# Two attention layers and two gated MLPs on one core: queries written over their normalised tile, a P ring of 48 places, other ranks for norms and spatial sums

## The chip, the core and the metric

The kernel runs on one core of a Trainium2 chip. The metric is the device time of one execution in microseconds. The core has five instruction streams: TensorE (PE, with its weight loads shown as PEld), VectorE (DVE), ScalarE (ACT), GpSimd (POOL) and SyncE (SP), which starts the DMAs. They meet only at semaphores.

## The reference

Two layers, each an attention with 32 query heads of 16 that share one key and one value head, and a gated MLP whose gate mixes the 2048 tokens. `x` is 2048 x 512, bf16.

```python
def _A_ref(x, wq, wk, wv, wo):
    q = (x @ wq).reshape(B, S, H, Dh).transpose(0, 2, 1, 3)
    k = x @ wk
    v = x @ wv
    scores = jnp.einsum('bhqd,bkd->bhqk', q, k) * Dh ** (-0.5)
    p = _softmax(scores, axis=-1)
    o = jnp.einsum('bhqk,bkd->bhqd', p, v)
    return o.transpose(0, 2, 1, 3).reshape(B, S, H * Dh) @ wo

def _B_ref(x, w_in, w_sp, b_sp, w_out):
    z = _gelu(jnp.einsum('bsd,df->bsf', x, w_in))
    z1 = z[..., :Fh].copy()
    z2 = _layernorm(z[..., Fh:], axis=-1)
    g = jnp.einsum('ts,bsf->btf', w_sp, z2) + b_sp[None, :, None]
    return jnp.einsum('bsf,fd->bsd', z1 * g, w_out)

x = x + _A_ref(_layernorm(x), wq, wk, wv, wo)
x = x + _B_ref(_layernorm(x), w_in, w_sp, b_sp, w_out)
# the same two lines once more
```

## The kernel before

The program is written by a planner that runs on the host when the kernel is built. Work is cut into tasks, each with an engine, a modelled duration, dependencies and a priority (a smaller number goes first). `Sched` and `Kernel.run` walk through modelled time: whenever an engine is free, its `step_` function picks a ready task by priority, and that fixes the engine's instruction order and its semaphore waits. The chip then runs the five fixed streams. So a constant of the planner doesn't cost anything by itself; it changes the order of instructions.

**Attention.** The tokens are 16 tiles of 128 (t). `attn_inputs` makes, for each tile, a layer norm, its transpose, keys and values (`keys`, L766 on) and queries (`queries`, L795). The transposed norm `xnT(t)` lies in z1, in rows that the MLP fills only later: `z1[:, t // 4, 0:4, o:o + 128]`. The query matmuls (L800) read it, and an eviction (L810 on VectorE, L811 on ScalarE) writes the scaled queries to a ring Q of 8 tiles. A query job for t of 2 and more may start only when the layer's ramp is over (`full`), and for t of 8 and more only when all score blocks of tile t - 8 have been issued (`later`).

Queries are worked off in eight chunks (`CHUNKS`, 128 to 512 tokens), in 32 units of 512 columns for a layer. A unit meets 16 key tiles with 4 row groups each, so a layer has 2048 score blocks of 128 x 512. `issue_pack` (L1244) sends up to four blocks as one pack of score matmuls (L1286), each to a PSUM bank of its own; there are eight banks. A block then goes one of two ways. On ScalarE, `pick_exp` joins one or two blocks whose banks and whose places in the P ring are neighbours into one exponential (L1494): a single is 128x512, a pair 128x1024. Or on VectorE (task "A", priority 1.0): L1408 reads the bank and writes a first integer tile, and GpSimd or VectorE make two more from it (L1413), so that such a block takes three places of P. `issue_pack` gives VectorE a share of 0.32 or 0.34 of the blocks. All these tiles live in the ring `Pb` of `NPS` = 40 places, until the matmuls of P and V (L1549) have read them; `do_pv` sends those in rounds of four column groups, and `pv_hurry` sends them with fewer once under 8 places are free.

`pack_ready` (L1206) decides whether a pack may go: with fewer than four blocks only if ScalarE's modelled backlog is no more than `ACT_LOW`, and with no fewer than `FILL_MIN` (in layer 1's ramp `FILL_R`, with a backlog of 0). Score packs come first on TensorE, then P·V rounds, then everything else by priority.

**What lies between the score packs.** When a chunk is through, `attn_out` (L844) normalises, multiplies with wo, adds to X and makes the second layer norm (`ln`, statistics L638 and L639 on VectorE, then GpSimd), with priority 0.8. `mlp_in` forms a batch for each group of chunks: gelu on ScalarE (L1022, L1077) between two table loads, from matmuls L1017 and L1063. `spatial` (L1102) runs the token mix in five passes; passes 0 to 3 add up in `gp` with matmuls L1124 and an addition on VectorE (L1132, priority 1.05), 28 jobs a pass. The last pass and the output matmuls (L1162, L1170, L1191, L1195) come after all score blocks of the layer.

So the run has five stages: a start, the attention of layer 0 with the passes between its score packs, the change of layers, the attention of layer 1, and a tail.

Of the kernel before, what the change touches and what calls it, by code (L numbers as in the profile page):

```python
# [292 lines left out]
class Attn:  # L293

    def __init__(self, K, layer):
        self.K = K
        self.layer = layer
        self.kdep, self.vdep, self.qdep = {}, {}, {}
        self.nxt = 0
        self.started = False  # L300
        self.full = False
        self.ugs = []
        for ci, (q0, nq) in enumerate(CHUNKS):
            ng = 512 // nq
            for g0 in range(0, 4, ng):
                for half in range(2):
                    self.ugs.append(UG(ci, q0, nq, g0, ng, half))
        self.blocks = []
        nrot = K.NROT[layer]
        for kt in range(NT):  # L310
            for u in self.ugs[:nrot]:
                self.blocks += [(u, kt, j) for j in range(4)]
        for u in self.ugs[nrot:]:
            self.blocks += [(u, kt, j) for kt in range(NT) for j in range(4)]
        self.nrot = nrot
        self.end = None
        self.last_block = {}
        for i, (u, kt, j) in enumerate(self.blocks):
            for t in range(u.q0 // P, (u.q0 + u.nq) // P):
                self.last_block[t] = i + 1  # L320
        self.chunk_ugs = {}
        for u in self.ugs:
            self.chunk_ugs.setdefault(u.ci, []).append(u)
# [69 lines left out]
class Kernel:  # L393
# [1 line left out]
    SCORE_CAP = 6  # L395
    WSP_FROM = 25000
    W_FROM = 45000
    NPS = 40
    QT = 8
    PV_FREE = 6  # L400
    KT_ACT = 16
    CREDIT = 2
# [22 lines left out]
    PE_LINE = 5000  # L425
    WARM = 0.6
    FILL_MIN = 2
    FILL_R = 4
    NOID = (False, True)
    PTT = 1.8  # L430
    ACT_LOW_R = 0
    PV_R = 0
    RAMP_SHARE1 = 0.0
    ACT_LOW = 1300
    POOL_MAX = 1400
    DVE_MAX = 1500
    DVE_HIGH = 1800
# [41 lines left out]
    def alloc(self):  # L479
        nc = self.nc  # L480
        ps = self.es.enter_context(nc.psum_tensor("ps_all", [P, 4096], FP32))
        self.ps32 = ps[:].rearrange("p (b c) -> p b c", c=512)
        self.ps16 = ps[:].bitcast(BF16).rearrange("p (b c) -> p b c", c=1024)
        self.ident = self.sb([P, P], BF16, "ident")
        self.zero = self.sb([P, 32], BF16, "zero")
        self.ident16 = self.sb([P, P], FP16, "ident16")
        self.X = self.sb([P, NT, D], BF16, "X")
        self.kT = self.sb([P, 2, S], BF16, "kT")
        self.NV = 1 + len(TERMS)
        self.V = self.sb([P, self.NV, NT, 32], BF16, "V")  # L490
        self.wq = self.sb([P, KD, D], BF16, "wq")
        self.wk0 = self.sb([P, KD, DH], BF16, "wk0")
        self.wk = self.sb([P, KD, 8, DH], BF16, "wk")
        self.wv = self.sb([P, KD, DH], BF16, "wv")
        self.wo = self.sb([P, 4, D], BF16, "wo")
        self.w_in = self.sb([P, KD, FF], BF16, "w_in")
        self.w_out = self.sb([P, NF, D], BF16, "w_out")
        self.Q = self.sb([P, 4, self.QT * P], BF16, "Q")
        self.xnT2 = self.sb([P, 1, KD, 512], BF16, "xnT2")
        self.z2 = self.sb([P, 8, FH], BF16, "z2")  # L500
        self.z1 = self.sb([P, 4, NF, 512], BF16, "z1")
        self.gp = self.sb([P, 4, NF, 512], FP16, "gp")
        self.wstr = self.sb([P, self.NWS, 512], BF16, "wstr")
        self.bspc = self.sb([P, 512], BF16, "bspc")
        self.oT = self.sb([P, 3, 512], BF16, "oT")
        self.o_norm = self.sb([P, 4, 512], BF16, "o_norm")
        self.onT = self.sb([P, 4, 4, P], BF16, "onT")
        self.rden = self.sb([P, 2, 32], FP32, "rden")
        self.NXN = 4
        self.xn = self.sb([P, self.NXN, D], BF16, "xn")  # L510
        self.ln_st = self.sb([P, NT, 6], FP32, "ln_st")
        self.ln_mv = self.sb([P, NT, 2], FP32, "ln_mv")
        self.ln_rs = self.sb([P, NT, 1], FP32, "ln_rs")
        self.ln_nm = self.sb([P, NT, 1], FP32, "ln_nm")
        self.nm2 = self.sb([P, NT, 1], FP32, "nm2")
        self.st2 = self.sb([P, NT, 2, 6], FP32, "st2")
        self.mv2 = self.sb([P, NT, 2], FP32, "mv2")
        self.rs2 = self.sb([P, NT, 1], FP32, "rs2")
        self.masks = self.sb([P, 2], FP32, "masks")
        self.dummy = self.sb([P, 4], FP32, "dummy")  # L520
        self.vw = self.sb([P, self.NV], FP32, "vw")
        self.mhalf = self.sb([P, 1], FP32, "mhalf")
        self.Pb = self.sb([P, self.NPS, 512], BF16, "Pb")
        self.Pi = self.Pb[:].bitcast(I16)
# [33 lines left out]
    def misc_cap(self):  # L558
        if self.batch is not None:
            return 2  # L560
        if not self.attn_on():
            return 7
        return 1 if self.attns[self.ai].full and self.pe_line() < self.CAP_LINE else 2

    def score_cap(self):
        return self.SCORE_CAP if self.attns[self.ai].full else 4

    def job(self, prio, pieces, consumers, tag, kind="misc", batch=None, spare=0, only=None):

# [222 lines left out]
        made, outs = self.job(prio, [(kf, c_mm(8, 96), [dep, self.t_wk, self.ldv])], [mk, mkv], "KV")  # L792
        return made, outs[0], outs[1]

    def queries(self, A, t, dep, war, prio):  # L795
        def qf(e, b, lo, hi):
            ins = None
            for g in range(lo, hi):
                for kd in range(KD):
                    ins = e.matmul(self.ps32[:, b, g * P:(g + 1) * P], self.wq[:, kd, g * P:(g + 1) * P], self.xnT(t, kd),  # L800
                                   start=(kd == 0), stop=(kd == KD - 1))
            return ins

        def mk(last, bank):
            o = self.Q[:, :, t % self.QT * P:(t % self.QT + 1) * P]

            def src():
                return self.ps32[:, bank(), :].rearrange("p (g c) -> p g c", g=4)
            return Task(None, None, None, [last] + list(war), prio - 0.5, tag="qev",
                        alts={"dve": (c_ps(512), lambda e: e.tensor_scalar(o, src(), QSCALE, None, op0=ALU.mult)),  # L810
                              "act": (c_act(512), lambda e: e.activation(o, src(), ACTF.Copy, scale=QSCALE))})  # L811
        def later():

            if self.ai >= len(self.attns) or not self.attns[self.ai].full:
                return False
            return t < self.QT or A.nxt >= A.last_block[t - self.QT]
        made, outs = self.job(prio, [(lambda e, b: qf(e, b, 0, 2), c_mm(8, 128), [dep, self.ldq]),
                                     (lambda e, b: qf(e, b, 2, 4), c_mm(8, 128), [])], [mk], "Q", only=later if t >= self.Q_LATE else None)
        return made, outs[0]

    def attn_inputs(self, layer, xdeps):
# [5 lines left out]
        for t in range(NT):  # L827
# [6 lines left out]
            made, kout, vout = self.keys(t, ev, war, pr)  # L834
            A.kdep[t] = [kout]
            A.vdep[t] = [vout]
            m, q = self.queries(A, t, ev, war, pr + 0.01 if t < 2 else 4 + 0.05 * t if t < self.QT else 3 + 0.02 * t)
            A.qdep[t] = q
            self.xnT_use[t] = made + m
        self.attns.append(A)  # L840
# [3 lines left out]
    def attn_out(self, A, ci):  # L844
# [127 lines left out]
        buf = 0  # L972
        base = next(CHUNKS[g[0]][0] for g in GROUPS if ci in g)
        evs = []
        allx = self.ln(tl, [xnew[t] for t in tl], 0.8, pool=not last)
        for a in range(0, ntl, 2):
            pair = tl[a:a + 2]
            xs = allx[a:a + 2]
# [123 lines left out]
    def spatial(self, B, pi, final):  # L1102
# [5 lines left out]
        for tc in range(4):  # L1108
# [6 lines left out]
            else:  # L1115
# [4 lines left out]
                for f in range(NF):  # L1120
# [8 lines left out]
                    def mk(lp, bank, f=f, tc=tc):  # L1129
                        src = self.bspc[:] if pi == 0 else self.gp[:, tc, f, :]  # L1130
                        dps = [lp, lb] + self.gp_free if pi == 0 else [lp, B.gpw[(tc, f)]]
                        return Task("dve", c_ps(512), lambda e: e.tensor_tensor(  # L1132
                            self.gp[:, tc, f, :], self.ps32[:, bank(), :], src, ALU.add), dps, 1.05, tag="gp")
                    made, outs = self.job(self.SP_PRIO + 0.1 * pi, pcs, [mk], "SP%d" % pi)
                    B.gpw[(tc, f)] = outs[0]
                    if pi == 0:
# [69 lines left out]
    def pack_ready(self):  # L1206
# [2 lines left out]
        A = self.attns[self.ai]  # L1209
        av = self.banks.avail()  # L1210
        room = min(4, len(av), self.score_cap() - self.score_held)
        low = self.ACT_LOW if A.full or A.layer == 0 else self.ACT_LOW_R
        if room < (self.FILL_MIN if A.full or A.layer == 0 else self.FILL_R) or room < 4 and self.act_backlog() > low:
            return None
        blks = []
        deps = []
# [6 lines left out]
        if not blks or len(blks) < room and len(blks) < 4 and A.nxt + len(blks) < len(A.blocks) and self.act_backlog() > low:  # L1223
            return None
        return A, blks, deps, av

    def act_backlog(self):
        return max(0.0, self.s.free["act"] - self.s.t) + 450.0 * len(self.act_q)
# [15 lines left out]
    def issue_pack(self, A, blks, deps, bs):  # L1244
# [36 lines left out]
        def fn(e):  # L1281
            ins = None
            for i, (u, kt, j) in enumerate(blks):
                o = u.q0 % (self.QT * P)
                q = self.Q[32 * j:32 * j + 32, u.g0:u.g0 + u.ng, o:o + u.nq]
                ins = e.matmul(self.ps32[:, jb[i].i, :], self.kT[32 * j:32 * j + 32, u.half, kt * P:(kt + 1) * P], q,  # L1286
                               tile_position=(32 * j, 0), start=True, stop=True)
            return ins
# [338 lines left out]
    def pack_due(self):  # L1627
# [15 lines left out]
        d = max(t, s.free["dve"]) + 130  # L1643
        known += [d + 603 * (i + 1) for i in range(sum(1 for _, _, k in s.arm["dve"] if k.start is None and k.tag == "A"))]
        known.sort()
        e2 = known[self.FILL_MIN - 1] if len(known) >= self.FILL_MIN else t + 600
        e4 = known[3] if len(known) > 3 else t + 1e5
        dry = max(t, s.free["act"]) + 450.0 * len(self.act_q) - self.ACT_LOW
        w = min(e4, max(e2, dry))
        if w > t:  # L1650
            s.event(w)
# [274 lines left out]
```

## Time and profile before

| | us |
|---|---|
| median of five runs | 1583.33 |
| lowest and highest | 1580.65, 1587.83 |
| the profiled execution | 1583.63 |
| its span, first to last instruction | 1581.5 |
| TensorE busy | 1490.6 (94%) |
| ScalarE busy | 1431.3 (90%) |
| VectorE busy | 1385.9 (88%) |
| GpSimd busy | 1043.6 (66%) |
| score matmuls L1286, 4096 | 591.9 |
| P·V matmuls L1549, 6668 | 520.9 |
| spatial matmuls L1124, 840 | 214.1 |
| query matmuls L800, 512 | 41.2 |
| VectorE score blocks L1408, 1286 | 840.1 |
| spatial sums L1132, 224 | 151.5 |

Busy time is the union of an engine's instructions, so overlapping ones are counted once. A group's line gives busy time and mean duration of one, then the idle time of the engine just before its instructions and whom it waited for. The granted TensorE clock was 0.986 in the mean, lower only in the first 75 us. ScalarE's instructions overlap when they follow each other directly, so the mean duration of an exponential is more than the time that one more of them takes.

### The profile page before, as it was taken

The page shows a single profiled execution, that of the slowest core. Times are in us where ns is not written, and L with a number is a line of the kernel's source. Part 1 is how long each engine was busy: PE and PEld are TensorE (multiplying, and loading weights), DVE is VectorE, ACT ScalarE, POOL GpSimd, SP SyncE. Part 2 cuts the span into 40 slices and gives each one's busy share as a digit, 9 for nine tenths or more (in the row PEclk, how much of TensorE's full clock was granted, in tenths as well). Part 3 has the DMA queues.
Part 4 walks back from the last instruction along what each step waited for, and adds up shares of the span by engine and source line. Part 5 has one row for each costly group of instructions (what it writes and reads, how often), then busy time and mean ns, then how long its engine had stood idle before and what let it go on. Part 6 is the DMA issues. An engine that isn't in the chain of part 4 may idle for free.

```text
span 1581.5 us, 36212 instructions
## 1 busy us (share of the span) xinstructions
PE 1490.6 (94%) x13992; PEld 499.6 (32%) x13992; DVE 1385.9 (88%) x2627; ACT 1431.3 (90%) x2063; POOL 1043.6 (66%) x1269
## 2 busy tenths in 40 slices
PE   6999899999999999999998989999999999999999
PEld 3232232222322223223543322322233222322345
DVE  7799978999899997898965999799998899889888
ACT  6899989999999999997479999999999999999950
POOL 5577767777677776774103767576776777677727
PEclk8699999999999999999999999999999999999999
DMA  6300000010000020110210000010011011101012
GB/s 132 96 9 8 2 15 18 18 33 17 15 15 15 15 41 1 23 36 19 41 35 18 8 5 8 8 31 18 18 28 15 15 28 24 18 15 28 18 34 64
DMA packets 123991, 39.71 MB, mean 25 GB/s; under 512 B 116272, under 2 KB 123312, under 8 KB 123824
## 3 DMA queue, kind: packets, MB, share of 16 engines
q1 hardware_dynamic: 123824, 37.41, 11.0%
q8 instruction: 114, 1.87, 0.5%
q14 instruction: 53, 0.43, 0.1%
HBM read 6.98 MB, written 2.10 MB: 6 GB/s over the span
## 4 chain that ended last, share of the span: by engine, by line
ACT 54%; PE 33%; DVE 8%; issue 3%; DMA 1%; POOL 1%; SPq 0%; ACTq 0%
ACT Pb L1494 53%; PE ps_all L1286 8%; PE ps_all L1549 8%; PE ps_all L1124 5%; DVE Pb L1408 3%; PE ps_all L1063 3%; PE ps_all L1017 3%; PE ps_all L1191 2%; DMA z<-xn 1%; DVE Pb L1413 1%; PE ps_all L961 1%; DVE gp L1132 1%; PE ps_all L800 1%; DVE ln_st L638 1%; ACT L1736 1%
## 5 line engine op out<-in xcount | busy, mean ns | idle before, releaser
L1494 ACT ACTIVATE Pb<-ps_all 128x1024 bf16<-128x1024 f32 (+1 forms) x1890 | 1336.9, 891 | 40.7 <-PE ps_all L1286 36.8
L1413 POOL TENSOR_SCALAR Pb<-Pb 128x1024 int16<-128x1024 int16 (+1 forms) x1022 | 900.1, 881 | 331.4 <-DVE Pb L1413 195.2
L1408 DVE TENSOR_SCALAR Pb<-ps_all 128x512 int16<-128x512 f32 x1286 | 840.1, 683 | 94.1 <-PE ps_all L1286 83.1
L1286 PE MATMUL ps_all<-Q,kT 32*128 32x512 bf16 x4096 | 591.9, 389 | 62.4 <-ACT Pb L1494 32.9
L1549 PE MATMUL ps_all<-Pb,V 128*32 128x512 bf16 x6668 | 520.9, 389 | 3.1 <-ACT Pb L1494 1.7
L1286 PEld LDWEIGHTS ps_all<-Q,kT 32*128 32x128 bf16 x4096 | 153.6, 91 | 596.3 <-ACT Pb L1494 373.0
L1124 PE MATMUL ps_all<-wstr,z 128*128 128x512 bf16 x840 | 214.1, 381 | 4.7 <-POOL z L1045 1.5
L1413 DVE TENSOR_SCALAR Pb<-Pb 128x1024 int16<-128x1024 int16 (+1 forms) x493 | 190.4, 418 | 9.2 <-PE ps_all L1549 7.2
L1549 PEld LDWEIGHTS ps_all<-Pb,V 128*32 128x32 bf16 x6668 | 120.0, 95 | 214.6 <-issue 118.4
L1132 DVE TENSOR_TENSOR gp<-ps_all,gp 128x512 f16<-128x512 f32 x168 | 112.9, 686 | 20.8 <-PE ps_all L1124 19.6
L1124 PEld LDWEIGHTS ps_all<-wstr,z 128*128 128x128 bf16 x840 | 67.3, 97 | 105.4 <-DVE Pb L1408 16.6
L629 POOL TENSOR_SCALAR ln_rs<-ln_mv 128x1 f32<-128x1 f32 (+2 forms) x48 | 10.5, 224 | 97.0 <-DVE ln_mv L639 91.2
L1191 PE MATMUL ps_all<-w_out,z 128*128 128x512 bf16 x224 | 56.1, 380 | 0.7 <-DVE V L790 0.3
L859 DVE CAST oT<-ps_all 128x512 bf16<-128x512 f32 x64 | 43.7, 684 | 14.1 <-PE ps_all L1549 13.7
L1017 PE MATMUL ps_all<-w_in,xnT 128*128 128x448 bf16 x256 | 53.1, 353 | 1.4 <-DVE Pb L1408 1.2
L1063 PE MATMUL ps_all<-xnT,w_in 128*128 128x512 bf16 (+2 forms) x280 | 51.5, 337 | 0.0
L1030 DVE BATCH_NORM_STATS2 st<-z 128x6 f32<-128x448 bf16 x64 | 35.8, 602 | 13.6 <-ACT z L1022 13.5
L1077 ACT ACTIVATE z<-ps_all 128x512 bf16<-128x512 f32 (+1 forms) x60 | 31.1, 572 | 17.1 <-PE ps_all L1063 17.1
L1132 DVE TENSOR_TENSOR gp<-ps_all,bspc 128x512 f16<-128x512 f32 x56 | 38.6, 688 | 8.3 <-PE ps_all L1124 7.9
L638 DVE BATCH_NORM_STATS2 ln_st<-X 128x6 f32<-128x512 bf16 x64 | 43.3, 681 | 2.0 <-DMA X<-in_A_x_dram 1.8
L629 POOL TENSOR_SCALAR rs<-mv 128x4 f32<-128x4 f32 (+2 forms) x10 | 2.3, 233 | 61.4 <-DVE mv L1032 61.4
L800 PE MATMUL ps_all<-z,wq 128*128 128x128 bf16 x512 | 41.2, 225 | 0.6 <-DVE Pb L1408 0.2
(69 smaller groups left out, 700.4 us busy)
## 6 DMA issues: line engine op xcount, KB each, us to landing
out_dram<-X SPq DMA_DIRECT2D x16, 128.0 KB, 1.7
w_in<-in_B_w_in_dram SPq DMA_DIRECT2D x1, 1792.0 KB, 7.7
X<-in_A_x_dram SPq DMA_DIRECT2D x3, 512.0 KB, 6.6
bspc<-in_B_b_sp_dram SPq DMA_DIRECT2D x8, 128.0 KB, 3.3
w_out<-in_B_w_out_dram SPq DMA_DIRECT2D x1, 896.0 KB, 9.6
wstr<-in_B_w_sp_dram SPq DMA_TRANSPOSE x40, 4.1
X<-in_A_x_dram SPq DMA_DIRECT2D x2, 256.0 KB, 3.3
wq<-in_A_wq_dram SPq DMA_DIRECT2D x1, 512.0 KB, 4.4
```

Source lines behind the costliest of these rows:

```text
L638: a = self.dve(c_ps(512), lambda e, t=t: e.bn_stats(st[:, t, :], X[:, t, :]), [dep], prio, tag="lnst")
L800: ins = e.matmul(self.ps32[:, b, g * P:(g + 1) * P], self.wq[:, kd, g * P:(g + 1) * P], self.xnT(t, kd), start=(kd == 0), stop=(kd == KD - 1))
L1017: ins = e.matmul(self.ps32[:, b, 0:448], self.xnT2[:, buf, kd, o:o + P], self.w_in[:, kd, FH + h * 448:FH + (h + 1) * 448], start=(kd == 0 ...
L1063: ins = e.matmul(self.ps32[:, b, i * nq:(i + 1) * nq], self.w_in[:, kd, f * P:(f + 1) * P], self.xnT2[:, buf, kd, 0:nq], start=(kd == 0), ...
L1124: ins = e.matmul(self.ps32[:, b, :], self.z2[:, (s0 + i) % 8, f * P:(f + 1) * P], self.wstr[:, sl[i // 4][1] + i % 4, :], start=(i == 0), ...
L1132: return Task("dve", c_ps(512), lambda e: e.tensor_tensor(self.gp[:, tc, f, :], self.ps32[:, bank(), :], src, ALU.add), dps, 1.05, tag="gp")
L1191: ins = e.matmul(self.ps32[:, b, :], self.z1[:, tc, f, o:o + P], self.w_out[:, f, :], start=(f == 0), stop=(f == NF - 1))
L1286: ins = e.matmul(self.ps32[:, jb[i].i, :], self.kT[32 * j:32 * j + 32, u.half, kt * P:(kt + 1) * P], q, tile_position=(32 * j, 0), start=T ...
L1408: return lambda e: e.tensor_scalar(self.Pi[:, dst():dst() + k, :], self.ps32[:, bank:bank + k, :], EBIAS + lo, lo, op0=ALU.add, op1=ALU.max)
L1413: return lambda e: e.tensor_scalar(self.Pi[:, dst():dst() + k, :], self.Pi[:, src():src() + k, :], lo, 1.0, op0=ALU.add, op1=ALU.mult)
L1494: return e.activation(self.Pb[:, s0:s0 + n, :], self.ps32[:, b0:b0 + n, :], ACTF.Exp, scale=ESCALE)
L1549: ins = e.matmul(self.ps32[32 * j:32 * j + 32, u.bank.i, :], self.V[:, var, kt, :], self.Pb[:, sl.i, :], tile_position=(0, 32 * j), start= ...
```

## The change

- The ring Q is gone. The eviction of the queries of tile t writes them to `xnT(t)`, the tile that they were made from, and the score matmuls read them in z1. Since the key matmuls read the same tile, the eviction now depends on them too. The condition on tile t - 8 goes, and with it `last_block`.
- The P ring grows from 40 to 48 places (8 KB for each partition, as much as Q had).
- The query jobs of tiles 8 to 15 get priority 4 + 0.05 t in place of 3 + 0.02 t.
- The second norm of every chunk but the last gets 1.1 in place of 0.8, behind VectorE's score blocks (1.0); the additions of the spatial passes get 0.95 in place of 1.05, ahead of them.
- `ACT_LOW` is 1200 in place of 1300, `FILL_R` 3 in place of 4. Some constants become functions of the backlog on TensorE.

```diff
@@ Attn.__init__ @@
         self.end = None
-        self.last_block = {}
-        for i, (u, kt, j) in enumerate(self.blocks):
-            for t in range(u.q0 // P, (u.q0 + u.nq) // P):
-                self.last_block[t] = i + 1
@@ Kernel @@
-    NPS = 40
-    QT = 8
+    NPS = 48
...
     FILL_MIN = 2
-    FILL_R = 4
+    FILL_LINE = 3000
+    MISC_RAMP = 2
+    LN2_PRIO = 1.1
+    GP_P = 0.95
+    SCORE_RAMP = 4
+    FILL_BUSY = 2
+    ACT_LOW_BUSY = 1200
+    FILL_R = 3
...
-    ACT_LOW = 1300
+    ACT_LOW = 1200
...
-        self.Q = self.sb([P, 4, self.QT * P], BF16, "Q")
@@ misc_cap, score_cap @@
-        return 1 if self.attns[self.ai].full and self.pe_line() < self.CAP_LINE else 2
+        A = self.attns[self.ai]
+        if not A.full and A.layer:
+            return self.MISC_RAMP
+        return 1 if A.full and self.pe_line() < self.CAP_LINE else 2
...
-        return self.SCORE_CAP if self.attns[self.ai].full else 4
+        A = self.attns[self.ai]
+        return self.SCORE_CAP if A.full else self.SCORE_RAMP if A.layer else 4
@@ queries @@
-            o = self.Q[:, :, t % self.QT * P:(t % self.QT + 1) * P]
+            o = self.xnT(t)
...
-            if self.ai >= len(self.attns) or not self.attns[self.ai].full:
-                return False
-            return t < self.QT or A.nxt >= A.last_block[t - self.QT]
+            return self.ai < len(self.attns) and self.attns[self.ai].full
@@ attn_inputs @@
-            m, q = self.queries(A, t, ev, war, pr + 0.01 if t < 2 else 4 + 0.05 * t if t < self.QT else 3 + 0.02 * t)
+            m, q = self.queries(t, ev, war + made, pr + 0.01 if t < 2 else 4 + 0.05 * t)
@@ attn_out @@
-        allx = self.ln(tl, [xnew[t] for t in tl], 0.8, pool=not last)
+        allx = self.ln(tl, [xnew[t] for t in tl], 0.8 if last else self.LN2_PRIO, pool=not last)
@@ spatial @@
-                            self.gp[:, tc, f, :], self.ps32[:, bank(), :], src, ALU.add), dps, 1.05, tag="gp")
+                            self.gp[:, tc, f, :], self.ps32[:, bank(), :], src, ALU.add), dps, self.GP_P, tag="gp")
@@ pack_ready; pack_due uses the same two functions @@
-        low = self.ACT_LOW if A.full or A.layer == 0 else self.ACT_LOW_R
-        if room < (self.FILL_MIN if A.full or A.layer == 0 else self.FILL_R) or room < 4 and self.act_backlog() > low:
+        low = self.act_low() if A.full or A.layer == 0 else self.ACT_LOW_R
+        if room < (self.fill_min() if A.full or A.layer == 0 else self.FILL_R) or room < 4 and self.act_backlog() > low:
...
+    def busy_pe(self):
+        return self.pe_line() > self.FILL_LINE
+
+    def fill_min(self):
+        return self.FILL_BUSY if self.busy_pe() else self.FILL_MIN
+
+    def act_low(self):
+        return self.ACT_LOW_BUSY if self.busy_pe() else self.ACT_LOW
@@ issue_pack @@
-                o = u.q0 % (self.QT * P)
-                q = self.Q[32 * j:32 * j + 32, u.g0:u.g0 + u.ng, o:o + u.nq]
+                o = u.q0 % 512
+                q = self.z1[32 * j:32 * j + 32, u.q0 // 512, u.g0:u.g0 + u.ng, o:o + u.nq]
```

## The prediction

> **What bounds the kernel now.** I read four views in this order: busy time by stage, who waited for whom, the chain of work that ended last, and the groups by form; then a piece of ScalarE's timeline for the price of one exponential. The first cuts the span where ScalarE's work changes: start (to 75 us), attention of layer 0 (to 742), change of layers (to 853), attention of layer 1 (to 1521), tail.
>
> ```profile
> 75.00:742.00 667.00, 637.41 (x6038) 198.56 (x6036) 597.76 (x1102) 649.37 (x943) 485.83 (x564) 1.00 0.08 17
> 742.00:853.00 111.00, 100.53 (x994) 50.61 (x990) 77.76 (x173) 69.66 (x105) 14.40 (x37) 1.00 0.18 38
> 853.00:1521.00 668.00, 634.00 (x6057) 197.70 (x6055) 603.64 (x1125) 652.66 (x937) 474.38 (x555) 1.00 0.09 17
> 1521.00:1581.50 60.50, 57.55 (x389) 30.20 (x387) 51.65 (x91) 4.93 (x9) 29.94 (x32) 1.00 0.26 64
> ```
>
> After the length come the busy times of TensorE, its weight loads, VectorE, ScalarE and GpSimd. In both attention stages ScalarE is idle for only 667 - 649.4 = 17.6 us and 668 - 652.7 = 15.3 us, 33 us together; TensorE is at 95%, VectorE at 90%. Those 1335 us are ScalarE's, with the two others close behind. In the tail ScalarE has nothing and TensorE 57.6 of 60.5 us.
>
> ```profile
> PEld ps_all L1286 <- ACT Pb L1494: 373.0, 863, 1.3
> PEld ps_all L1286 <- DVE Pb L1408: 120.0, 286, 1.3
> DVE Pb L1408 <- PE ps_all L1286: 83.1, 164, 5.4
> ACT Pb L1494 <- PE ps_all L1286: 36.8, 74, 3.1
> POOL Pb L1413 <- PE ps_all L1549: 21.6, 53, 2.4
> PEld ps_all L1286 <- DVE gp L1132: 18.1, 42, 0.5
> DVE Pb L1413 <- PE ps_all L1549: 7.2, 19, 0.7
> DVE Pb L1408 <- PE ps_all L1549: 1.7, 6, 0.7
> ACT Pb L1494 <- PE ps_all L1549: 0.7, 2, 0.4
> ```
>
> Columns: total us, times, longest. The PSUM cycle is visible: score matmuls (L1286) wait for the exponentials (L1494) and VectorE blocks (L1408) that free banks. A full P ring would show as producers waiting for the P·V matmuls (L1549): ScalarE 0.7 us, VectorE 8.9, the 66% busy GpSimd more. So the present ring of 40 hardly stops ScalarE directly; what it does to the planner's pairing is not shown.
>
> ```profile
> ACT 54%; PE 33%; DVE 8%; issue 3%; DMA 1%; POOL 1%; SPq 0%; ACTq 0%
> ...
> L1494 ACT ACTIVATE Pb<-ps_all 128x1024 bf16<-128x1024 f32 x920 | 939.4, 1105 | 27.3 <-PE ps_all L1286 24.4 <-PE ps_all L1549 0.4
> L1494 ACT ACTIVATE Pb<-ps_all 128x512 bf16<-128x512 f32 x970 | 568.4, 688 | 13.4 <-PE ps_all L1286 12.3 <-PE ps_all L1549 0.3
> ...
> L810 DVE TENSOR_SCALAR Q<-ps_all 128x512 bf16<-128x512 f32 x30 | 20.4, 682 | 1.1 <-PE ps_all L800 1.1
> ...
> 813.73 2.00 ACT L1494 ACTIVATE Pb<-ps_all 128x1024 bf16<-128x1024 f32 x3 [0.66 <-PE ps_all L1286]
> 816.24 2.07 ACT L1494 ACTIVATE Pb<-ps_all 128x512 bf16<-128x512 f32 x4 [0.50 <-PE ps_all L1286]
> ```
>
> The chain runs over ScalarE for 54%. There are 920 pairs and 970 single exponentials. The last two lines give the price of not pairing: four blocks as one pair and two singles take 2.00 us, as four singles 2.07, so joining two singles saves about 0.06 us.
>
> **The change, part by part**, against the profiled execution's 1583.63 us (span 1581.5; median of the runs 1583.33, so no correction). First what is not a change: FILL_BUSY, ACT_LOW_BUSY, MISC_RAMP and SCORE_RAMP give the values used before, so the new `busy_pe` branches decide nothing.
>
> *Queries into the normalised tile.* The same 512 matmuls and 32 evictions remain; the copy's source and place change, not its shape. The added dependency (`war + made`) is on key matmuls of the same engine, which come before the query matmuls anyway. What moves is time: tiles 8 to 15 no longer wait until the ring place of tile t - 8 is used up. By the windows of L800, ten tiles of layer 0 were done by 150 us, two fell in 175 to 200 and four in 350 to 425; layer 1 has two in 950 to 1000 and four in 1150 to 1200. So about six tiles a layer move forward: 32 matmuls of two tiles take 2.48 us, so 7.4 us of TensorE, and 6 x 0.60 (0.68 less the overlap) = 3.6 us of VectorE. *Where they arrive* (100 to 225 us), TensorE is busy 114.8 of 125 and VectorE 116.8: 10.2 and 8.2 us free, so 0; without that cover each eviction puts off a score block, 2 x 3.6 = +7.2 us. *Where they leave*, ScalarE is idle 75 - 73.64 = 1.4 us and 50 - 48.59 = 1.4 us; half of it back is -1.4 (0 to -2.8). Tiles 8 to 15 also drop in priority, from 3.16 to 3.30 to 4.4 to 4.75, behind the spatial passes at 3.5 and more; what hides that is the gap before the first pass at about 230 us, some 100 us after they may start.
>
> *P ring of 48.* Direct waits: ScalarE's 0.7 us whole, and a quarter of VectorE's 8.9, since VectorE holds only 8% of the chain: -3 (0 to -9.6). Longer drain at a layer's end: 8 more tiles are two rounds of four, 0.22 us each, +0.9 at most. Pairing: 5% of 970 singles are 24 pairs x 0.06 = -1.5; if half of the 485 possible pairs came, -14.5; as many lost, +1.5. I stay near the small end, because odd numbers of blocks in a pack make singles whatever the ring has.
>
> The Trainium skill ("ScalarE: Activation LUTs", What ACT_TABLE_LOAD costs) puts an ACTIVATE at 186 ns + 0.833 ns an element, of which back-to-back ones overlap by about 93 ns; each joined pair would save 93 ns, and this term would be -2.2 in place of -1.5. The trace's 2.00 against 2.07 us says 60 to 70 ns, and the sum goes by it.
>
> *ACT_LOW from 1300 to 1200.* Part packs wait until ScalarE's modelled backlog is 0.1 us shorter, so fewer and fuller packs, and more risk of running dry. ScalarE waits for scores 5.0 us and 5.7 us in the two attention stages, and 74 times in all: +7.4 if each grows by 0.1, -5 if half goes; I take -1.
>
> *Spatial sums above score blocks (0.95 against 1.0).* The 224 additions of 0.61 us (ten in 6.09 us) free their bank sooner; score weights now wait 18.1 us for it, the spatial ones 4.9. A tenth is -2; -5 at best. Against: a score block queued behind the addition is 0.6 us later, and the score matmuls wait for its bank; ScalarE's waits in attention (10.7 us) could grow by half, +5. In the change of layers the additions also go ahead of layer 1's first norms; about eight fall after 766, 8 x 0.6 = +4.8 at most, 0 taken, since they have to be done there anyway.
>
> *Second norms behind score blocks (1.1).* 30 norms x (0.68 + 0.17) = 25.6 us of VectorE no longer come ahead of blocks: -1. Queued behind is each norm's xn on GpSimd, its transposing DMA on SP and a chunk's gelu batch; the exponentials hide the batch. Only the group that feeds the last large pass has no cover: two blocks, +1.2 a layer, +2.4.
>
> *FILL_R from 4 to 3* acts in layer 1's ramp alone (778 to 853 us): packs of three when ScalarE is empty. It idles some 0.6 us ahead of most groups there. Three blocks a gap in place of four cost 128/3 - 128/4 = 11 more gaps, +6.6; 20 earlier starts of 0.17 us are -3.4. After 838 ScalarE is continuous, with the last keys in: 0 taken.
>
> Sum: -1.4 - 3 - 1.5 - 1 - 2 - 1 = -9.9, so 1583.63 - 9.9 = 1573.7; I forecast **1574**.
>
> **Rivals.** *Nothing reaches the end:* ScalarE's work (2810 blocks) and the shares of the engines are untouched, 33 us of idle in attention is mostly waiting for gelu matmuls, and the tail is TensorE's. For it: the 0.7 us. Against: TensorE and VectorE are a few per cent from being the bound, so small reliefs count. Time 1583.
>
> *VectorE's score blocks come late:* 224 additions go ahead of them, in the attention stages, where VectorE is 90% busy. Each holds a score bank 0.6 us longer, which ScalarE feels wherever its backlog is below that. If one in eight opens a gap, 28 x 0.6 = 17 us, less the other gains of 8: 1583.6 + 17 - 8 = 1592.6, say 1592. It decides from the point where gaps outweigh the other gains of 7.9 us, 13 of 224. For it: scores already wait 120 us for these blocks and ScalarE has a thinner reserve now. Against: ScalarE waited for scores only 38 times in attention, and the same additions had to run before.
>
> *The ring was what kept singles single:* half the pairs come (-14.5 in place of -1.5): 1574 - 13 = 1561. For it: in 150 to 225 us the tiles made and not yet consumed, counted from the trace, come to 30 to 40 of 40. Against: singles also stand in the ramp, where the ring is far from full.
>
> **How the numbers follow.** Forecast 0.45 (its own range 1566 to 1579), large gain 0.14, nothing 0.16, late blocks 0.25. About 0.3%, 4.75 us, is what a measurement can tell from no change, so faster means below 1578.6 and slower above 1588.1. Forecast and large gain make faster 0.59; a twentieth of that lands above 1578.6 but is balanced by part of "nothing" below it. Same is 0.16, slower 0.25. The range runs from just under the large gain, 1559, to late blocks at 1592, which leaves about 0.18 outside; the low ends of all terms together (-41) and the high ones (+36) would need every term at its end at once.
>
> **What would show it.** Right: L800 all before 225 us in layer 0 and before 1025 in layer 1; waits on L1549 near 0 for VectorE and ScalarE; ScalarE's idle in the two attention stages under 33 us; L1494 with about 940 pairs; start, change of layers and tail within 2 us each. Wrong: more waits of L1494 for L1286 than 10.7 us in attention (late blocks), fewer pairs or fewer L1408 than 1286 (work moved onto ScalarE), or a change of layers longer than 111 us (norms behind additions, packs of three).

## The result, and the profile after

The changed kernel takes 1584.33 us (median of 44 runs) against 1582.42 us (79 runs of the kernel before, in the same comparisons). The ratio is 1.0016, with a 95% interval of 1.0009 to 1.0023: about 2.5 us slower (the two medians differ by 1.9 us). That is a small loss clear of 1, and inside the 0.3% that counts as no change here. The forecast of 9.9 us less did not come; the rival "nothing reaches the end" (1583 us) did. Line numbers move: score matmuls are now L1299, exponentials L1507, VectorE score blocks L1421 and L1426, P·V L1562, spatial matmuls and sums L1128 and L1136, queries L805.

Busy time by stage of the changed kernel, in the columns and stretches shown for the kernel before (length, then TensorE, weight loads, VectorE, ScalarE, GpSimd, TensorE's granted clock, DMA share, GB/s):

```profile
75.00:742.00 667.00, 634.70 (x6051) 197.48 (x6049) 594.37 (x1096) 648.37 (x947) 480.44 (x555) 1.00 0.08 17
742.00:853.00 111.00, 102.89 (x969) 50.11 (x970) 79.61 (x173) 67.57 (x91) 14.05 (x36) 0.96 0.21 38
853.00:1521.00 668.00, 631.44 (x6068) 196.83 (x6066) 601.82 (x1106) 652.87 (x943) 480.84 (x549) 1.00 0.09 17
1521.00:1581.50 60.50, 58.67 (x403) 30.65 (x400) 52.85 (x94) 5.64 (x10) 29.91 (x32) 1.00 0.23 62
```

ScalarE is idle for 18.6 and 15.1 us in the two attention stages, 33.8 us together against 33.0 before; the signs had it under 33. TensorE and VectorE do become less busy there (TensorE by 2.7 and 2.6 us, VectorE by 3.4 and 1.8), and it changes nothing for ScalarE. New is the clock, third from the end: 0.96 in the change of layers.

Who waited for whom in the changed kernel (total us, times, longest):

```profile
PEld ps_all L1299 <- ACT Pb L1507: 376.3, 857, 1.5
PEld ps_all L1299 <- DVE Pb L1421: 119.7, 278, 1.3
DVE Pb L1421 <- PE ps_all L1299: 86.0, 164, 5.1
ACT Pb L1507 <- PE ps_all L1299: 34.4, 76, 1.9
POOL Pb L1426 <- PE ps_all L1562: 20.7, 52, 2.1
PEld ps_all L1299 <- DVE gp L1136: 15.0, 36, 0.5
DVE Pb L1426 <- PE ps_all L1562: 3.2, 11, 0.6
DVE Pb L1421 <- PE ps_all L1562: 1.3, 5, 0.6
```

Each local aim is met a little. VectorE's waits for places of P (L1562) fall from 8.9 to 4.5 us and ScalarE's 0.7 us are gone; the wait of score weights for spatial sums falls from 18.1 to 15.0. The first two lines, the PSUM cycle of score matmuls and ScalarE, stay within 1%. The same wait for ScalarE, where it falls on the score matmuls themselves and not on their weight loads, grows from 32.9 to 44.2 us, so TensorE waits more for ScalarE than before, not less.

The groups by form of the changed kernel, and below them, from the same view, those of the experiment with its ring back at 40 places:

```profile
L1507 ACT ACTIVATE Pb<-ps_all 128x1024 bf16<-128x1024 f32 x924 | 944.2, 1110 | 27.9 <-PE ps_all L1299 23.9 <-POOL Pb L1426 0.4
L1507 ACT ACTIVATE Pb<-ps_all 128x512 bf16<-128x512 f32 x965 | 566.1, 702 | 11.0 <-PE ps_all L1299 10.6
L1421 DVE TENSOR_SCALAR Pb<-ps_all 128x512 int16<-128x512 f32 x1283 | 836.1, 684 | 96.5 <-PE ps_all L1299 86.0 <-PE ps_all L1562 1.3
```

```profile
L1507 ACT ACTIVATE Pb<-ps_all 128x1024 bf16<-128x1024 f32 x958 | 968.6, 1098 | 24.3 <-PE ps_all L1299 19.9 <-PE ps_all L1562 0.7
L1507 ACT ACTIVATE Pb<-ps_all 128x512 bf16<-128x512 f32 x895 | 525.2, 681 | 11.7 <-PE ps_all L1299 10.1 <-PE ps_all L1562 1.3
```

Four pairs more than before (924 against 920), three VectorE blocks fewer: ScalarE's work is what it was (all exponentials together 1336.7 us, 1336.9 before). And the smaller ring has the more pairs, so the ring was not what kept singles single.

Where the queries went, busy time of the query matmuls L805 in the changed kernel (TensorE, weight loads, clock, DMA):

```profile
75.00:150.00 75.00, 15.51 (x204) 11.22 (x202) 1.00 0.04 9
150.00:225.00 75.00, 0.88 (x13) 0.53 (x10) 1.00 0.02 5
225.00:742.00 517.00, 0.00 (x0) 0.00 (x0) 0.99 0.09 19
```

As forecast, all are done by 225 us. The two stretches that they left, all engines of the changed kernel:

```profile
350.00:425.00 75.00, 69.62 (x674) 20.11 (x673) 69.30 (x131) 73.64 (x103) 52.92 (x55) 1.00 0.12 24
1150.00:1200.00 50.00, 45.09 (x458) 12.51 (x456) 48.63 (x93) 49.74 (x67) 36.55 (x39) 1.00 0.19 33
```

TensorE is relieved by 2.1 us (71.73 before) and 3.2 us (48.29 before). ScalarE has the same 73.64 us in the first stretch, to the hundredth, and 1.15 us more in the second, of the 1.4 us that it was idle there.

### The profile page after: what moved, and what is told of

The parts are those of the page before. It is cut to its first block, busy times and chain, and to the rows that moved or that the text cites. A ratio compares the mean times of both kernels' runs of the same rounds, so it can differ in the third digit from the quotient of the medians.

```text
span 1582.8 us, 36207 instructions
## 1 busy us (share of the span) xinstructions
PE 1487.6 (94%) x14030; PEld 497.6 (31%) x14030; DVE 1385.9 (88%) x2608; ACT 1431.0 (90%) x2062; POOL 1046.3 (66%) x1257
## 4 chain that ended last, share of the span: by engine, by line
ACT 53%; PE 37%; DVE 4%; issue 3%; DMA 1%; POOL 1%; SPq 0%; ACTq 0%; POOLq 0%
ACT Pb L1507 52%; PE ps_all L1299 9%; PE ps_all L1562 9%; PE ps_all L1128 6%; PE ps_all L1021 3%; PE ps_all L1067 3%; PE ps_all L1195 3%; DVE Pb L1421 2%; PE ps_all L805 1%; PE ps_all L965 1%; DVE gp L1136 1%; ACT L1750 1%; DMA z<-xn 1%; PE ps_all L1166 1%; PE ps_all L775 1%
## 5 line engine op out<-in xcount | busy, mean ns | idle before, releaser
L1507 ACT ACTIVATE Pb<-ps_all 128x1024 bf16<-128x1024 f32 (+1 forms) x1889 | 1336.7, 902 | 38.9 <-PE ps_all L1299 34.4
L1426 POOL TENSOR_SCALAR Pb<-Pb 128x1024 int16<-128x1024 int16 (+1 forms) x1010 | 902.1, 893 | 317.8 <-DVE Pb L1426 179.5
L1421 DVE TENSOR_SCALAR Pb<-ps_all 128x512 int16<-128x512 f32 x1283 | 836.1, 684 | 96.5 <-PE ps_all L1299 86.0
L1299 PE MATMUL ps_all<-z,kT 32*128 32x512 bf16 x4096 | 586.6, 388 | 70.5 <-ACT Pb L1507 44.2
L1562 PE MATMUL ps_all<-Pb,V 128*32 128x512 bf16 x6662 | 517.6, 388 | 2.7 <-ACT Pb L1507 0.8
L1299 PEld LDWEIGHTS ps_all<-z,kT 32*128 32x128 bf16 x4096 | 151.4, 91 | 600.5 <-ACT Pb L1507 376.3
L1128 PE MATMUL ps_all<-wstr,z 128*128 128x512 bf16 x840 | 214.6, 383 | 2.4 <-DVE Pb L1421 0.4
L1426 DVE TENSOR_SCALAR Pb<-Pb 128x1024 int16<-128x1024 int16 (+1 forms) x477 | 187.8, 425 | 5.0 <-PE ps_all L1562 3.2
L1562 PEld LDWEIGHTS ps_all<-Pb,V 128*32 128x32 bf16 x6662 | 120.5, 95 | 213.3 <-issue 116.0
L1136 DVE TENSOR_TENSOR gp<-ps_all,gp 128x512 f16<-128x512 f32 x168 | 112.7, 686 | 22.4 <-PE ps_all L1128 21.3
L1128 PEld LDWEIGHTS ps_all<-wstr,z 128*128 128x128 bf16 x840 | 68.1, 98 | 103.9 <-DVE Pb L1421 16.3
L1021 PE MATMUL ps_all<-w_in,xnT 128*128 128x448 bf16 x256 | 54.0, 353 | 0.7 <-ACT Pb L1507 0.3
L1067 PE MATMUL ps_all<-xnT,w_in 128*128 128x512 bf16 (+2 forms) x280 | 51.5, 337 | 0.1
L1136 DVE TENSOR_TENSOR gp<-ps_all,bspc 128x512 f16<-128x512 f32 x56 | 38.6, 689 | 6.4 <-PE ps_all L1128 5.8
L635 POOL TENSOR_TENSOR ln_rs<-ln_rs,mhalf 128x1 f32<-128x1 f32 (+2 forms) x48 | 29.4, 616 | 17.9 <-DVE Pb L1426 15.0
```

Of the source, the lines that this page charges most:

```text
L1021: ins = e.matmul(self.ps32[:, b, 0:448], self.xnT2[:, buf, kd, o:o + P], self.w_in[:, kd, FH + h * 448:FH + (h + 1) * 448], start=(kd == 0 ...
L1067: ins = e.matmul(self.ps32[:, b, i * nq:(i + 1) * nq], self.w_in[:, kd, f * P:(f + 1) * P], self.xnT2[:, buf, kd, 0:nq], start=(kd == 0), ...
L1128: ins = e.matmul(self.ps32[:, b, :], self.z2[:, (s0 + i) % 8, f * P:(f + 1) * P], self.wstr[:, sl[i // 4][1] + i % 4, :], start=(i == 0), ...
L1136: return Task("dve", c_ps(512), lambda e: e.tensor_tensor(self.gp[:, tc, f, :], self.ps32[:, bank(), :], src, ALU.add), dps, self.GP_P, ta ...
L1421: return lambda e: e.tensor_scalar(self.Pi[:, dst():dst() + k, :], self.ps32[:, bank:bank + k, :], EBIAS + lo, lo, op0=ALU.add, op1=ALU.max)
L1426: return lambda e: e.tensor_scalar(self.Pi[:, dst():dst() + k, :], self.Pi[:, src():src() + k, :], lo, 1.0, op0=ALU.add, op1=ALU.mult)
```

## The experiments

Two theories were stated first. A: no part reaches the end, because ScalarE's work stays. B: the parts have effects of 5 us and more that cancel. A third, C, came from the profiles of the first eight runs and is explained below. Ratios are to the kernel before, run beside each experiment.

**One part undone at a time.** The edits, each alone in the changed kernel:

```diff
# a_ring40
-    NPS = 48
+    NPS = 40
# a_ln2
-    LN2_PRIO = 1.1
+    LN2_PRIO = 0.8
# a_gp
-    GP_P = 0.95
+    GP_P = 1.05
# a_qgate: queries() and attn_inputs(); last_block as in the kernel before
-            return self.ai < len(self.attns) and self.attns[self.ai].full
+            if self.ai >= len(self.attns) or not self.attns[self.ai].full:
+                return False
+            return t < 8 or A.nxt >= A.last_block[t - 8]
...
-            m, q = self.queries(t, ev, war + made, pr + 0.01 if t < 2 else 4 + 0.05 * t)
+            m, q = self.queries(A, t, ev, war + made, pr + 0.01 if t < 2 else 4 + 0.05 * t if t < 8 else 3 + 0.02 * t)
# a_low
-    ACT_LOW_BUSY = 1200
+    ACT_LOW_BUSY = 1300
...
-    ACT_LOW = 1200
+    ACT_LOW = 1300
# a_fillr
-    FILL_R = 3
+    FILL_R = 4
```

> The changed kernel with its P ring back at 40 places, all else as changed. Theory A (no part reaches the end, because ScalarE's work stays and its idle in attention is mostly not waiting for what the parts move): ratio to before 0.997 to 1.003, pairs of exponentials within 5% of 924. Theory B (the parts have effects of 5 us and more that cancel; the ring is the one that gains): 1.005 or more, fewer pairs, and more VectorE and GpSimd waits on the P.V matmuls than in the changed kernel.

> The changed kernel with the second norms back at priority 0.8. Theory A: ratio to before 0.997 to 1.003. Theory B with this part as a gain of 1 us, as forecast: nothing visible either, 1.001 to 1.004; with it as the loser: 0.996 or less.

> The changed kernel with the spatial sums back behind the score blocks (1.05). Theory A: ratio to before 0.997 to 1.003. Theory B with this part as the loser that eats the others' gain (the rival of late score blocks): 0.995 or less, and ScalarE waits less for score matmuls than the changed kernel's 34.4 us.

> The changed kernel with the queries still written over their normalised tile, but released and ranked as before (tile t from 8 on only when the blocks of tile t - 8 are issued, priority 3 + 0.02 t). Theory A: ratio to before 0.997 to 1.003. Theory B with the early queries as a loser (VectorE's evictions ahead of score blocks at 75 to 225 us): 0.995 or less; as the gain that was forecast (1.4 us): 1.002 to 1.004.

> The changed kernel with ACT_LOW and ACT_LOW_BUSY at 1300 as before. Theory A: ratio to before 0.997 to 1.003. Theory B with this part as a loser (ScalarE runs dry more often): 0.995 or less and ScalarE's wait for score matmuls well under 34.4 us; as a gainer: 1.005 or more with more score packs of two.

> The changed kernel with FILL_R back at 4. Theory A: ratio to before 0.997 to 1.003, and the time from the last exponential of layer 0 to the end of layer 1's ramp as before. Theory B with packs of three as the loser (the changed kernel's profile has TensorE at half clock for some microseconds in that ramp): 0.995 or less, no half clock between 740 and 855 us.

**Two controls**, in which a constant without a meaning of its own moves by 5 ns, in the changed kernel and in the kernel before. The planner then fixes another order:

```diff
# a_slack, b_slack
-    SLACK = 280
+    SLACK = 285
```

> Control: the changed kernel with the planner's constant SLACK at 285 in place of 280 ns, a step with no meaning of its own. It makes another order of instructions. Theory A, with the order's own scatter as the measure: some ratio between 0.995 and 1.005 to before, and as far from the changed kernel as the undone parts are. Theory B: within 0.1% of the changed kernel (1.0006 to 1.0026), since no part was undone.

> Control: the kernel before with SLACK at 285 in place of 280 ns and nothing else. Theory A, with the order's own scatter as the measure: a ratio away from 1 by 0.1 to 0.5% in either direction. Theory B: 0.999 to 1.001.

| kernel | ratio to before | 95% interval | full speed lost: first 75 us, later | in all, mean of the runs |
|---|---|---|---|---|
| before (profile shown) | 1 | | 20.5, 1.7 | 19.3 |
| changed (profile shown) | 1.0016 | 1.0009 to 1.0023 | 15.4, 6.8 | 22.0 |
| a_ring40 | 1.0012 | 0.9999 to 1.0025 | 13.7, 8.5 | 20.6 |
| a_ln2 | 1.0033 | 1.0021 to 1.0044 | 17.1, 3.4 | 21.3 |
| a_gp | 1.0009 | 0.9997 to 1.0022 | 12.0, 13.7 | 26.2 |
| a_qgate | 0.9991 | 0.9980 to 1.0002 | 12.0, 3.4 | 19.7 |
| a_low | 1.0100 | 1.0085 to 1.0114 | 12.0, 22.2 | 31.6 |
| a_fillr | 1.0088 | 1.0069 to 1.0107 | 12.0, 6.9 | 24.5 |
| a_slack (control) | 1.0048 | 1.0031 to 1.0065 | 15.4, 5.2 | 27.3 |
| b_slack (control) | 1.0033 | 1.0020 to 1.0046 | 12.0, 6.8 | 22.0 |

The fourth column is (1 - granted clock) x length in us, added over stretches of 4 us of the profile shown for each kernel; the last is (1 - mean granted clock) x span, averaged over the runs (127 of the kernel before, 44 of the changed kernel, 4 to 12 of the others). One profile can mislead: that of a_slack is the fastest of its 11 runs, that of a_low the slowest of its 4.

The controls decide how the rest may be read. A step that means nothing moved the kernel before by 0.33% and the changed one by 0.32% (1.0048 against 1.0016). So the ring, the norms, the spatial sums and the query release, whose undoing moved the changed kernel by -0.25 to +0.17%, each count for no more than a shuffle. ACT_LOW and FILL_R stand out: with either undone it is 0.84 and 0.72% slower. Those two are not what theory A expected, and B finds support in them. (The norms' 1.0033 also lies just above A's 1.003, but no further from the changed kernel than the control does.) But the undone differences don't add up: taking the six as gains and losses of the parts, +0.04 (ring), -0.17, +0.07, +0.25, -0.84 and -0.72 make -1.37%, where the six together made +0.16%. The kernel before has both constants at their old values and is as fast as the changed one. Undoing one constant gives another order altogether, not the same order less one part; that the two gain in this order and other parts lose as much is not excluded.

**The clock.** a_low's profile shows where a part of its time went. Its chain of work that ended last (start, length, what):

```profile
1011.18 0.77 POOL xn L657
...
1011.98 3.96 DMA xnT<-xn
...
1015.98 0.93 PE ps_all L1021 x2
```

and the same place in the busy times of all engines:

```profile
1010.00:1014.00 4.00, 3.34 (x34) 0.82 (x31) 4.00 (x8) 4.00 (x7) 2.79 (x4) 1.00 0.35 70
1014.00:1016.00 2.00, 0.41 (x3) 0.12 (x4) 1.94 (x4) 2.00 (x4) 1.26 (x2) 0.78 0.00 0
1016.00:1024.00 8.00, 8.00 (x46) 1.31 (x46) 4.30 (x8) 4.64 (x7) 2.69 (x3) 0.50 0.00 0
```

TensorE stands behind a transposing DMA of a second norm and is busy for 0.41 of 2 us. Its clock falls to 0.50 and stays there for 8 us, in which ScalarE has work for only 4.64. The planner's durations know a full clock only. Another part is not the clock's: this order has 875 pairs and 1062 singles in place of 924 and 965, and its exponentials take 1342.8 us in place of 1336.7. The changed kernel's clock is down at two places as well, behind gaps of 0.94 and 1.38 us; first its own clock there, then that of the kernel before:

```profile
736.00:742.00 6.00, 5.81 (x37) 1.31 (x35) 3.10 (x5) 5.01 (x9) 2.60 (x5) 0.52 0.02 4
840.00:849.00 9.00, 7.99 (x76) 2.44 (x76) 1.11 (x4) 7.23 (x9) 0.00 (x0) 0.62 0.00 1
```

```profile
736.00:742.00 6.00, 5.41 (x54) 1.48 (x54) 5.39 (x11) 6.00 (x10) 3.92 (x8) 1.00 0.01 1
840.00:849.00 9.00, 6.82 (x92) 1.94 (x88) 0.00 (x0) 8.98 (x15) 0.00 (x0) 1.00 0.00 0
```

That gave theory C: the changed order leaves TensorE idle in lumps, and the half clock takes back what the order gains. Two repeats, with no edit, ask whether the drops belong to the order:

> The changed kernel once more, for a second profile. Theory C (the changed order leaves TensorE idle in lumps, its clock drops to half there, and that takes back what the order gains): the clock is below full again near 736 to 742 us and 840 to 850 us, some 5 to 9 us of full speed lost after the first 75 us. If the drops belong to the execution and not to the order: other places, or none.

> The kernel before once more, for a second profile. Theory C: as in its first profile, no more than some 3 us of full speed lost after the first 75 us, near 584 to 592 us. If the drops belong to the execution: other places or a loss as large as the changed kernel's.

They don't belong to it by place. The changed kernel's second profile has full clock at 736 to 742 and 840 to 849 us and drops at 164, 224, 1160 and 1516 us; the kernel before has them at 952 and 1512 instead of 584. By amount, after 75 us: 6.8 and 7.0 us lost in the changed kernel, 1.7 and 5.1 in the other; the start adds 15.4 and 20.5 to the one, 20.5 and 15.4 to the other, so that the first two profiles lose the same 22.2 us in all. So C in its first form, two fixed places in the change of layers, falls.

The clocks of all runs say more than four profiles. Among runs of one and the same kernel the time follows the loss: each us of full speed lost goes with 0.57 us of time in the changed kernel (44 runs, correlation 0.94) and 0.56 in the kernel before (127 runs, 0.87). The changed kernel loses 22.0 us in the mean (standard error 0.8), the other 19.3 (0.3; 18.4 to 21.1 in its five groups of runs). At 0.57 that is 1.5 us of time, and a line of this slope through the runs of each kernel leaves the changed one 1.3 us slower at an equal clock; together these are the 2.8 us by which the means of the runs differ. So the clock goes with about half of the loss, and it hides no gain of 9.9 us. This is read from runs as they fell, on different chips, and not set by an edit.

**The same order with the clock held up.** Into gaps on TensorE that the planner itself leaves, groups of four matmuls of zeros are put, which add zero to an open P·V bank; the order of all other instructions stays. The planner itself already puts such groups where its modelled TensorE is busy for less than 0.6 of the last 3.4 us: 24 of them in the kernel before, 35 in the changed one. a_fill2 differs from a_fill in the two constants, 260 and 0.92.

```diff
# a_fill; b_fill and the others are made in the same way
+    FILL_GAP = 300
+    FILL_ACT = 0.8
...
+    def filler(self, gap):
+        if gap < self.FILL_GAP or self.s.t < 20000 or not any(x.tag == "warm" for _, _, _, x in self.s.prog["pe"]):
+            return None
...
+        if not us or self.pe_activity() >= self.FILL_ACT:
+            return None
+        b = us[0].bank.i
+        n = max(1, int((gap - 200) // 216))
...
+        def fn(e):
+            for _ in range(n):
+                for j in range(4):
+                    e.matmul(self.ps32[32 * j:32 * j + 32, b, :], self.zero[:], self.wq[:, 0, :],
+                             tile_position=(0, 32 * j), start=False, stop=False)
...
```

> The changed kernel in its own order, with 121 extra groups of four matmuls of zeros put into the gaps of 0.3 us and more that its planner leaves on TensorE where its activity is low; they add zero to an open P.V bank. Theory C: under 3 us of full speed lost after the first 75 us (6.8 in the changed kernel's profile), ratio to before 0.996 to 0.999. Theory A (only the order counts, and the order is kept): 1.001 to 1.003, or more, by up to 121 x 0.22 us, if the gaps are not idle on the chip.

> The kernel before in its own order, with 105 such groups of zeros. Theory C: it loses only 1.7 us of full speed after the first 75 us, so there is little to win: ratio 0.998 to 1.001. Theory A: 1.000 or slower, like the changed kernel with its groups.

> The kernel with ACT_LOW back at 1300 (1.010 to before, 22 us of full speed lost after 75 us in its profile) with 108 groups of zeros in its gaps, order kept. If its 1% was the clock: under 4 us lost, ratio 0.998 to 1.003. If it was the order: 1.007 or more.

> The kernel with FILL_R back at 4 (1.0088 to before, 6.9 us lost after 75 us in its profile) with 126 groups of zeros, order kept. If the clock made its 0.9%: 0.998 to 1.002. If the order did, the clock giving only what it gave in the changed kernel (0.4%): 1.004 to 1.006.

> The control of the changed kernel (SLACK 285, 1.0048 to before) with 103 groups of zeros, order kept. If the scatter between orders is the clock's: within 0.15% of the changed kernel with its groups (0.9974). If it is the order's own: still 0.25% or more above it.

> The control of the kernel before (SLACK 285, 1.0033 to before) with 107 groups of zeros, order kept. If the scatter between orders is the clock's: within 0.15% of the kernel before with its groups (0.9982). If it is the order's own: 1.0005 or more.

> The changed kernel with the queries released and ranked as before (0.9991 to before) and 126 groups of zeros in its gaps, order kept. If the groups add to it what they gave the other five orders (0.2 to 0.7%): 0.992 to 0.997, the fastest so far. If its order already keeps the clock up (3.4 us lost after 75 us): 0.998 to 1.000.

> The changed kernel with 192 groups of zeros in place of 121 (gaps from 0.26 us, higher activity). If more groups hold the clock better, also in the first 75 us: 0.994 to 0.997. If the first 121 had already done it and the rest fill gaps that are needed (0.22 us each): 0.9975 to 1.003.

| order of | without zeros | with zeros | 95% interval | full speed lost with zeros | in all, mean of the runs |
|---|---|---|---|---|---|
| before | 1 | 0.9982 | 0.9969 to 0.9995 | 6.8, 0 | 6.6 |
| changed | 1.0016 | 0.9974 | 0.9961 to 0.9988 | 6.8, 1.7 | 8.4 |
| changed, 192 groups (a_fill2) | 1.0016 | 0.9974 | 0.9964 to 0.9985 | 6.8, 0 | 6.3 |
| a_qgate (q_fill) | 0.9991 | 0.9970 | 0.9961 to 0.9978 | 10.2, 0 | 8.4 |
| a_slack | 1.0048 | 0.9980 | 0.9969 to 0.9990 | 6.8, 1.7 | 10.6 |
| b_slack | 1.0033 | 1.0003 | 0.9992 to 1.0013 | 5.1, 5.3 | 8.4 |
| a_fillr | 1.0088 | 1.0022 | 1.0012 to 1.0032 | 5.1, 0 | 7.1 |
| a_low | 1.0100 | 1.0042 | 1.0027 to 1.0058 | 12.0, 10.2 | 15.2 |

All seven orders become faster, by 0.18 to 0.68%, though TensorE gets more work. The changed kernel with zeros shows both kinds of zero matmuls, those of the experiment (L1713) and the planner's own (L1691):

```profile
L1713 PE MATMUL ps_all<-wq,zero 128*32 128x512 bf16 x484 | 42.1, 388 | 0.0
L1691 PE MATMUL ps_all<-wq,zero 128*32 128x512 bf16 x140 | 13.9, 396 | 0.0
```

42 us of added TensorE time fit into gaps that were idle. So the half clock cost these orders at least the 3 to 11 us that the zeros gave back, and it is part of their scatter: the seven orders lie within 1.09% without and 0.72% with zeros. For the control of the changed kernel it was most of it (0.06% is left of 0.32), for the control of the kernel before less (0.21% of 0.33). The rest of the scatter is the order's own: a_fillr's profile with zeros loses nothing after 75 us, and the kernel is still 0.48% behind the changed one with zeros. That lies in a stage where FILL_R decides nothing: from the last exponential to the end it takes 66.2 us, the changed kernel with zeros 61.6. For a_low the clock is still down for 10 us of full speed, so the split of its 1% between clock, pairing and the rest stays open.

For the question of this study the pair that counts is the changed kernel with zeros against the kernel before with zeros: 0.9974 and 0.9982, 0.08% apart with intervals of 0.13 to 0.14% to each side. With the clock held up the change is still worth nothing that can be measured.

The fastest version is q_fill: the changed kernel with the queries released as before, and zeros in its gaps, 1577.52 us against 1582.32, ratio 0.9970 (0.9961 to 0.9978). It beats the kernel before and the changed one without zeros. From a_fill and b_fill its interval doesn't set it apart.

## Why the prediction was wrong

*Direction and sum.* The step that failed is the one written "Sum: -1.4 - 3 - 1.5 - 1 - 2 - 1 = -9.9": it let shares of waits on TensorE and VectorE (a half, a quarter, a tenth) reach the end, and added them as if each part acted alone. The runs showed neither. Measured was +2.5 us: the waits beside ScalarE shrank as told above, and ScalarE's idle in attention went from 33.0 to 33.8 us. The row "33 us together" was the bound on what such reliefs could return, and the prediction's own rival said what most of it was: waiting for gelu matmuls. They are still about half of it (8.4 and 8.3 us for L1067 and L1021 in the two stages, 10.4 and 8.2 before).

*Queries.* The move was forecast rightly: they are done by 225 us in layer 0, and all of layer 1's lie before 1025, as the list of signs had it. "0" where they arrive fits ScalarE, busy for 74.4 of 75 us from 100 to 175. The -1.4 where they leave is the term that shows the error most plainly: TensorE was freed, ScalarE's 73.64 us stayed. Undoing the early release made the kernel 0.25% faster, which is within a shuffle.

*Ring.* "Direct waits" halved (VectorE's to 4.5 us, where the signs had near 0) and were worth nothing that can be seen: 1.0012 with 40 places, 1.0016 with 48. Pairing, -1.5 and in the large rival -14.5, had the wrong cause: of 20 more pairs ("about 940") 4 came, the smaller ring has 958 and a_qgate 971, and the controls move by 15 and 24 with no rule on the ring touched (909 and 896).

*ACT_LOW and FILL_R* were given -1 and 0. Their undoing cost 0.84 and 0.72%, more than any bound that I had put on them (+7.4 and +6.6 us the other way; -5 and -3.4 for a gain). The bounds came from rows of ScalarE's waits; that another threshold leads to another order, with other pairs and other drops of the clock, was in none of them.

*Spatial sums and norms* (-2 and -1): the wait of score weights for a sum fell by 3.1 us; undone, 1.0009 and 1.0033. The rival of late score blocks didn't come: ScalarE waits for scores for 7.2 + 3.9 = 11.1 us in attention, 10.7 before. By its letter the sign of "more than 10.7" was met; 0.4 us is far from the 5 and 17 us that it stood for.

*What was missing altogether* is a term for the clock. The profile before was read with a mean granted clock of 0.986 and a low clock in the first 75 us only, and the prediction took it as fixed. There were 1.7 us of full speed lost after 75 us as well, at 584 to 592. Over the runs the changed order loses 2.6 us more, which by the line above is about 1.5 us of time, half of the measured loss; that the clock is its cause is read from the runs, not set by an edit.

What stays open: whether the changed rules are better or worse in the mean over many orders. Each kernel here is one order, and orders differ by 0.3% and more for a step that means nothing.

## What to carry to other kernels

Where a planner writes the order, move a constant without a meaning by a hair and time that before crediting any part: here it gave 0.33%, and no single part of the change but two threshold constants stood above it. Look at the granted clock of every run, not of one profile. Relief of an engine beside the bound is worth at most the bound engine's idle time that ends in a wait for it, so read that row first. Where the granted clock drops behind gaps, as it did here, a gap costs more than its own length; matmuls of zeros in gaps that are idle anyway are a cheap test of it.

## What the runs showed of the hardware

In the profile of a_low the clock fell within a gap of 1.5 us on TensorE and then stood at 0.50 for the whole 8 us shown, with TensorE busy for 8.00 of them. Every loss in the two columns read from profiles is a multiple of 1.7 us to within 0.2 us (1.7, 3.4, 5.1, 6.8 and so on to 22.2), as stretches of 3.4 us at half clock would give. The places differed between two profiles of the same kernel. The Trainium skill ("TensorE: Matmul & The Clock Gate", Part 1: The HAM clock gate) speaks of a free-running activity window and of counts that vary from run to run, which agrees with the moving places. It also has full speed return after one busy window of about 3.4 us, and that differs from the 8 us of a_low and from the start of these kernels. All engines of the kernel before in two stretches of the start and in a part of them, and then of the changed kernel with 192 groups of zeros in the two stretches:

```profile
24.00:50.00 26.00, 23.64 (x208) 7.78 (x204) 19.72 (x49) 20.40 (x28) 12.89 (x23) 0.63 0.45 84
50.00:75.00 25.00, 23.86 (x201) 6.63 (x200) 19.65 (x41) 21.80 (x34) 14.76 (x20) 0.70 0.41 136
48.00:56.00 8.00, 7.95 (x64) 2.26 (x56) 6.28 (x15) 6.12 (x10) 3.69 (x5) 0.50 0.31 84
```

```profile
24.00:50.00 26.00, 24.39 (x258) 8.44 (x255) 23.40 (x59) 24.16 (x32) 15.21 (x25) 0.86 0.50 103
50.00:75.00 25.00, 24.45 (x272) 7.80 (x269) 22.54 (x46) 24.70 (x36) 18.39 (x24) 1.00 0.35 117
```

The profile counts TensorE busy for 91 and 95% of the time, and its clock is 0.63 and 0.70; from 48 to 56 us it is busy for 99% at 0.50. So the busy share of the profile isn't what the clock follows; what is stays open here. With more zero matmuls, at busy shares of 94 and 98%, the clock is 0.86 and 1.00, and ScalarE gains 6.7 us of work in 51. Without zeros the ten kernels lost 12 to 20.5 us of full speed there, with zeros 5.1 to 12; this is the larger part of what the zeros returned to the kernel before, whose last exponential of layer 0 ends at 732.6 us in place of 742.1 (738.5 in its second profile), while the stretch from layer 1's first to its last exponential is 744.1 us in place of 742.0 (743.1).
